# ScalarE reads two PSUM banks in VectorE's place, and the first expert's shares are applied later

## The chip, the core and the metric

The kernel runs on one core of a Trainium2 chip. The metric is the device time of one execution in microseconds; several executions are given by their median. The engines are named as in the profile: PE (TensorE, matrix products), ACT (ScalarE), DVE (VectorE), POOL (GpSimd) and SP (SyncE, which here only issues DMAs). PE writes its sums into banks of PSUM; ACT and DVE read them from there.

## What is computed

Three stages, all in fp32. An attention with 2 batches, 8 heads, 768 tokens and a mask from clusters; then a softplus layer; then 8 experts, whose outputs are weighted by shares P that Sinkhorn's iteration makes:

```python
x = attention(q, k, v, centroids)                 # 1536 x 512
h = x @ w_in                                      # 512 -> 2048
x = (np.maximum(h, 0.0) + np.log1p(np.exp(-np.abs(h)))) @ w_out
P = np.exp(logits - logits.max())                 # logits = x @ w_gate, 1536 x 8
for _ in range(8):
    P /= P.sum(1, keepdims=True) + 1e-09
    P /= P.sum(0, keepdims=True) + 1e-09
    P *= N / E
for e in range(E):
    out += P[:, e:e + 1] * (np.maximum(x @ w1[e], 0.0) @ w2[e])
```

## The kernel before

**Precision.** Every fp32 operand is split into a rounded high part and its residue (names ending in h and l: wh/wl for weights, gh/gl for activations, vh/vl for second weights). A product takes three matrix passes: high x high, and the two mixed ones. ACT makes the high part by a cast, DVE or POOL the residue by a subtraction.

**Attention** runs to about 290 us and isn't touched by the change.

**Softplus layer**, about 290 to 580 us. `m1` lists 16 units of two chunks of the hidden dimension for one batch. `plain_group` makes a unit's four sums of 128 x 384 in the banks la and lb in turn, so a bank is used again by the group after next. After each sum `act` (L665 on) makes softplus: Abs (L671) reads the bank, Exp (L672) and Ln (L673) work on that in SBUF, DVE's L674 adds max(h, 0), which it reads from the bank, and ACT and DVE split the result (L676, L677). `layer2` multiplies the unit before. `fetch_unit` and `to32` convert the weights from 64-bit words on ACT and DVE in between (L123 to L127).

**Experts**, from about 580 us. Sixteen blocks k = 0 to 15, batch k // 8, expert k % 8. Both layers use one level of Strassen's method with seven products (Winograd's form): `PROD` lists them as pairs of an input combination and a weight combination, and which of two running sums, "a" or "b", each adds to. `l1_group` makes layer 1's products: for each quarter u of the hidden dimension, seven groups i of six passes. The running sum is read out between products: after groups 0, 2 and 3 ACT copies the bank to SBUF (L925, tiles c0 and c2); after groups 1, 4 and 5 DVE's L935 adds one of these copies to the bank and writes a block of the hidden layer (A11, A22, A12); after group 6 ACT writes A21 with Relu (L933). Group 6 adds to the bank that group 4's sum was read from, with only group 5 between. Three banks, la, lb and y1, take turns.

`l2_piece` makes layer 2's products, seven i in two halves p of three pieces each, in the banks y0/y2, y3, y4, y5, and DVE adds the finished pieces, times the share, onto the output in `xt` (L967 for the first, L969 for the rest). `g_sum` and `g_split` make the combinations of the hidden layer (L72, L74) and their residues (L897); `w2_load` (SP), `w2_add` (POOL's DMA queue) and `w2_split` (L875, L876) those of the weights; `w1_load` and `w1_split` (L845, L846) do it for layer 1. `t_step` builds sums of weights for later experts by DMAs in the same blocks. `first_share` doesn't exist.

**Order.** All of the third stage is put on one list by `do(t, ...)`: t counts steps, a step being one layer 1 group, 28 (G1) to a block. Layer 2 of block k lies beside layer 1 of block k + 1, from S0 = 28 (k + 1) on. For k = 0 it starts LAG0 = 8 steps later and is packed into the 20 steps left, since its sums need the shares: Sinkhorn (`sinkhorn`, phase 0 the row sums on DVE, phase 1 the column sums by a product with ones on PE, L767, and its division on DVE) has its eight iterations at 5.5 + 4.2 it, phase 1 2.9 steps after phase 0. The list gives the program's order; the scheduler of the framework orders each engine's queue by it, moved ahead by `high_priority(n)`, and an engine works through its queue strictly in order.

Of the kernel before, what the change touches and what calls it, by code (L numbers as in the profile page):

```python
# [7 lines left out]
F32 = mybir.dt.float32  # L8
# [3 lines left out]
AF = mybir.ActivationFunctionType  # L12
ALU = mybir.AluOpType
# [7 lines left out]
def attention_moe_moe2(ctx, tc, v, qt, kt, centroids, w_in, w_out, w_gate, w1, w2, eye, out, dbg=None):  # L21
    nc = tc.nc
    B, H, S, D = v.shape
    NC_ = centroids.shape[1]
    N, DM = out.shape
    DFF = w_in.shape[1]
    E = w_gate.shape[1]
    FE = w1.shape[2]
    P = 128
    NT = S // P  # L30
    HT = NT // 2
# [14 lines left out]
    xt = [xp.tile([P, KC, S], F32, tag=f"x{b}", name=f"x{b}") for b in range(B)]  # L46
# [533 lines left out]
    c2 = prep_centroids()  # L580
# [8 lines left out]
    for i in range(NHALF):  # L589
        g = i // 4  # L590
        for t in range(HT):
            n = 6 * i + 2 * t - LEAD
# [6 lines left out]
        for s in range(NT):  # L599
            n = 6 * i + s  # L600
# [37 lines left out]
    ps_y = ctx.enter_context(tc.tile_pool(name="ps_y", bufs=1, space=PSUM))  # L638
# [28 lines left out]
    def act(u, q, cols, src):  # L667
        nm = f"{u[0]}{u[1]}_{u[2]}_{u[3]}_{q}{cols.start}"
        g = GF[u, q][:, cols]
        t = fp.tile([P, FH], F32, tag="u", name="u" + nm, bufs=2)  # L670
        nc.scalar.activation(t, src, AF.Abs)  # L671
        nc.scalar.activation(t, t, AF.Exp, scale=-1.0)  # L672
        nc.scalar.activation(t, t, AF.Ln, bias=1.0)  # L673
        nc.vector.scalar_tensor_tensor(g, src, 0.0, t, ALU.max, ALU.add)  # L674
        gh, gl = GT[u, q]
        nc.scalar.copy(gh[:, cols], g)  # L676
        nc.vector.tensor_tensor(gl[:, cols], g, gh[:, cols].bitcast(F32), ALU.subtract)  # L677
# [38 lines left out]
    Pt = mp.tile([P, B * NT, E], F32, tag="Pt", name="Pt", bufs=1)  # L716
    Nt = mp.tile([P, B * NT, E], F32, tag="Nt", name="Nt", bufs=1)
# [36 lines left out]
    def sinkhorn(it, ph):  # L754
        n = B * NT
        if ph == 0:
            rs = mp.tile([P, n], F32, tag="rs", name=f"rs{it}", bufs=1)
            nc.vector.tensor_reduce(rs, Pt, AX.X, ALU.add)
            nc.vector.tensor_scalar(rs, rs, 1e-9, None, ALU.add)
            nc.vector.reciprocal(rs, rs)  # L760
            nc.vector.tensor_tensor(Pt, Pt, rs.unsqueeze(2).to_broadcast([P, n, E]), ALU.mult)
            cs = G["cs"] = mp.tile([P, E], F32, tag="cs2", name=f"cs{it}", bufs=1)
            nc.vector.tensor_reduce(cs, Pt.rearrange("p t e -> p e t"), AX.X, ALU.add)
            return
        cs = G["cs"]
        cp = ps_y.tile([P, E], F32, tag=f"y{4 + it % 2}", name=f"cp{it}")
        nc.tensor.matmul(cp, ones_f, cs, start=True, stop=True)  # L767
        nc.vector.tensor_scalar(cs, cp, 1e-9, float(E) / N, ALU.add, ALU.mult)
        nc.vector.reciprocal(cs, cs)
        nc.vector.tensor_tensor(Pt, Pt, cs.unsqueeze(1).to_broadcast([P, n, E]), ALU.mult)  # L770
        if it == 7:
            nc.vector.tensor_scalar(Nt, Pt, -1.0, None, ALU.mult)
# [108 lines left out]
    def x_tile(k, name, p):  # L881
        t = XG[k, name, p] = gp.tile([P, 2, FH], F32, tag="X" + name, name=f"X{name}{k}_{p}", bufs=XB[name])
        return t
# [18 lines left out]
    def l1_group(k, u, i):  # L902
        xn, wn, bank = PROD[i]
        p, v = divmod(u, 2)
        nm = f"{i}m{k}_{u}"
        if i in (0, 1, 3):
            tag = ("la", "lb", "y1")[(4 * k + u + (0, 1, 0, 2)[i]) % 3]
            LB[bank] = (ps_y if tag == "y1" else ps_l).tile([P, FH], F32, tag=tag, name="l" + nm)
        ps = LB[bank]
        hi, lo = XC[f"2_{k // E}", xn]  # L910
        wh, wl, s_ = W1U[k, u][wn]
        n, nk = 0, KC // 2
        for k_ in range(nk):
            ks = slice(k_ * P, (k_ + 1) * P)
            for wt, xx in ((wh, hi), (wh, lo), (wl, hi)):
                nc.tensor.matmul(  # L916
                    ps, wt[:, s_, ks], xx[:, k_, :],
                    start=i in (0, 1, 3) and n == 0, stop=n == 3 * nk - 1, skip_group_check=True,
                )
                n += 1  # L920
        if i in (0, 2, 3):
            tag = "c2" if i == 2 else "c0"
            c = LB["c", i] = gp.tile([P, FH], F32, tag=tag, name=tag + nm, bufs=1)
            with tc.high_priority(40):
                nc.scalar.copy(c, ps)  # L925
            return
        name = {1: "A11", 4: "A22", 5: "A12", 6: "A21"}[i]
        if not v:
            x_tile(k, name, p)
        t = XG[k, name, p]  # L930
        with tc.high_priority(40):
            if i == 6:
                nc.scalar.activation(t[:, v], ps, AF.Relu)  # L933
            else:
                nc.vector.tensor_tensor(t[:, v], ps, LB["c", {1: 0, 4: 3, 5: 2}[i]], ALU.add)  # L935
        if v and i != 6:
            nc.scalar.activation(t, t, AF.Relu, scale=1.0 if name == "A11" else -1.0)  # L937

    def l2_piece(k, i, p, t):
        sb, e = divmod(k, E)  # L940
        ch = PROD[i][2]
        if p == 0 and t == 0 and i in (0, 1, 3):
            tags = ("y4", "y5") if ch == "b" else (("y0", "y2")[k % 2], "y3")
            YA[ch] = [ps_y.tile([P, 512], F32, tag=g, name=f"Y{ch}{n}m{k}_{i}") for n, g in enumerate(tags)]
        y = YA[ch]
        ps = y[t // 2][:, t % 2 * 256 : t % 2 * 256 + 256]
        (gh, gl), (wh, wl) = GH[k, i, p], WH[k, i, p]
        ts = slice(t * P, (t + 1) * P)
        for v in range(2):
            for n, (g, w) in enumerate(((gh, wh), (gh, wl), (gl, wh))):  # L950
                nc.tensor.matmul(  # L951
                    ps, g[:, v, ts], w[:, v, :],
                    start=i in (0, 1, 3) and p == 0 and v == 0 and n == 0 and t != 1,
                    stop=p == 1 and v == 1 and n == 2, skip_group_check=True,
                )
        if p == 0 or t == 0:
            return
        r, c = ((0, 0), (0, 0), (0, 1), (1, 1), (1, 1), (0, 1), (1, 0))[i]
        yv = xt[sb].rearrange("p k s -> p (k s)").rearrange("p (m d) -> p m d", d=DM)
        for t_ in ((0, 1) if t == 1 else (2,)):  # L960
            m = r * HT + t_
            src = y[t_ // 2][:, t_ % 2 * 256 : t_ % 2 * 256 + 256]
            acc = yv[:, m, c * 256 : (c + 1) * 256]
            scl = (Nt if c else Pt)[:, sb * NT + m, e : e + 1]
            with tc.high_priority(30):
                if e == 0 and i in (0, 2, 3, 6):
                    nc.vector.tensor_scalar(acc, src, scl, None, ALU.mult)  # L967
                else:
                    nc.vector.scalar_tensor_tensor(acc, src, scl, acc, ALU.mult, ALU.add)  # L969
            if e == E - 1 and i in (5, 6):  # L970
                nc.sync.dma_start(out.rearrange("(b p t) d -> b t p d", b=B, t=NT)[sb, m], yv[:, m])

    def xc_prep(sb, step):
        blk, mq = XBLK[sb], slot_pool["mq"]
# [32 lines left out]
    def do(t, fn, *args):  # L1007
        ev2.append((t, len(ev2), fn, args))

    G1, LAG0, SH = 28, 8, 7  # L1010
    split_at = {}
    t1 = [G1 * k + (SH if k >= E else 0) for k in range(NB)]
    for k in range(NB):
# [12 lines left out]
            for name, d in (("+S1", 14), ("+S2", 17), ("+S3", 20.4)):  # L1026
                do(t1[k] + d, xc_prep, 1, (name,))
        S0 = t1[k] + G1
        lag = LAG0 if k == 0 else 0
        sp = (G1 - lag) / 14  # L1030
        for p in range(2):
            r = t1[k] + 16 if p == 0 else S0 + 0.3
            for n, name in enumerate(("S1", "S2", "S3")):
# [1 line left out]
            do(S0 + 7 + 2 * p, g_sum, k, "S4", p)  # L1035
        first = split_at.setdefault(k, [])
        for j in range(14):
            t = S0 + lag + sp * (j - 3) + 0.2 if j >= 4 else S0 + 2 * j - 5.8
            first.append(max(t, t1[k] + 9))
        for i in range(7):  # L1040
            b, i_ = divmod(7 * k + i - 3, 7)
            t = split_at[b][2 * i_ + 1] + 0.15 if b >= 0 else -1
# [3 lines left out]
        for j in range(14):  # L1046
            i, p = divmod(j, 2)
            do(first[j], w2_split, k, i, p)
            do(first[j] + 0.1, g_split, k, i, p)
            for n in range(3):  # L1050
                do(S0 + lag + sp * j + sp * n / 3 + 0.01, l2_piece, k, i, p, n)
    for c, jobs in enumerate(JM):
        for j, job in enumerate(jobs):
            for n in range(len(STEPS[job[0]])):
                do(2 + 14 * c + 46 * j + 4.4 * n, behind_pe, t_step, ("gp", "wp")[c], *job, n)
    for hf in range(2):
        do(0.5 + hf, lambda hf=hf: gate(1, hf))
        do(2.5 + 1.5 * hf, lambda hf=hf: gate_max(hf))
    for it in range(8):
        for ph in range(2):  # L1060
            do(5.5 + 4.2 * it + 2.9 * ph, lambda it=it, ph=ph: sinkhorn(it, ph))

    tsum_at = {}
    for c, jobs in enumerate(JF):
# [83 lines left out]
```

## Time and profile before

| | us |
|---|---|
| median of 3 executions | 1584.24 |
| lowest, highest | 1583.39, 1588.66 |
| the profiled execution | 1580.72 |
| its span, first to last instruction | 1578.9 |
| PE busy in it | 1501.3 (95%) |
| DVE busy | 1237.9 (78%) |
| ACT busy | 1005.9 (64%) |
| POOL busy | 775.8 (49%) |

The profile is of one execution. Busy time of PE is modelled from overlapping passes, so it is read through its waits: an entry "X <- Y" says that engine X stood idle before an operation, and that Y's end released it. The granted clock is the share of PE's full speed; 1.00 is 2.4 GHz and 0.50 is 1.2 GHz. L numbers are lines of the kernel before. A name like l0m<-chS,wlCm says which tile is written from which.

### The profile page before, as it was taken

The numbers are of one execution on the slowest core, as the hardware profiler recorded it, in microseconds if no ns is written. First come the engines' busy times: TensorE is split into PE (matmuls) and PEld (weight loads), VectorE is DVE, ScalarE is ACT, GpSimd is POOL, SyncE is SP. The second block draws the span as 40 slices with busy tenths as digits, with TensorE's granted clock in tenths as the row PEclk, the third lists the DMA queues.
The fourth block names the chain that finished last, engine by engine and source line by source line (L and its number), as shares of the span: only waits on it lengthen the run. The fifth ranks groups of instructions, "written<-read, shape, count | busy, mean of one in ns | idle before, by whom it ended". The sixth has DMA issues, their size and how long they took to land. (4 is left out here: it accounts for less than half of the span.)

```text
span 1578.9 us, 26984 instructions
## 1 busy us (share of the span) xinstructions
PE 1501.3 (95%) x9873; PEld 1436.7 (91%) x9873; DVE 1237.9 (78%) x1826; ACT 1005.9 (64%) x1854; POOL 775.8 (49%) x570
## 2 busy tenths in 40 slices
PE   5889999899999998999999999999999999999998
PEld 4778888789999868999999999988999999999998
DVE  4899899876764538887887787898878878878868
ACT  4788888766665535566656656675566666666664
POOL 3322323433223325466665666575556656656655
PEclk7999999899999999999999999999999999999999
DMA  8555520388886618879889798635646546545524
GB/s 226 146 148 137 145 66 6 97 235 222 209 216 159 147 47 188 226 178 263 202 210 254 184 227 208 155 107 141 185 131 149 139 141 149 139 142 147 141 89 109
DMA packets 268533, 253.02 MB, mean 160 GB/s; under 512 B 12272, under 2 KB 235632, under 8 KB 268400
## 3 DMA queue, kind: packets, MB, share of 16 engines
q1 hardware_dynamic: 229984, 205.09, 43.1%
q0 software_dynamic: 38272, 46.14, 18.4%
q8 instruction: 77, 1.26, 0.3%
q14 instruction: 56, 0.46, 0.1%
q10 hardware_dynamic: 144, 0.07, 0.0%
HBM read 202.49 MB, written 28.31 MB: 146 GB/s over the span
## 5 line engine op out<-in xcount | busy, mean ns | idle before, releaser
L876 POOL TENSOR_TENSOR vl<-w2r,vh 128x512 fp32r<-128x512 f32 x224 | 382.4, 1718 | 338.0 <-ACT vh L875 319.3
L897 DVE TENSOR_TENSOR gl<-XA,gh 128x768 fp32r<-128x768 f32 x160 | 165.5, 1036 | 80.1 <-ACT gh L896 79.5
L896 ACT CAST gh<-XA 128x768 fp32r<-128x768 f32 x160 | 133.9, 837 | 96.8 <-PE Ya1m L951 87.2
L875 ACT CAST vh<-w2r 128x512 fp32r<-128x512 f32 x224 | 137.6, 615 | 23.2 <-DMA w2r<-in_moe_w_dram 11.5
L951 PE MATMUL Ya0m<-vh,gl 128*128 128x256 f32 x512 | 144.3, 282 | 1.6 <-DVE gl L897 1.6
L951 PE MATMUL Ya0m<-vh,gh 128*128 128x256 f32 x512 | 144.1, 281 | 0.4 <-ACT gh L896 0.4
L951 PE MATMUL Ya0m<-vl,gh 128*128 128x256 f32 x512 | 144.0, 281 | 0.0
L554 DVE TENSOR_TENSOR el<-t,eh 128x384 fp32r<-128x384 f32 x192 | 102.5, 548 | 11.8 <-ACT eh L550 10.6
L951 PE MATMUL Yb0m<-vh,gh 128*128 128x256 f32 x384 | 109.1, 284 | 1.1 <-DVE x L969 1.1
L951 PE MATMUL Yb0m<-vh,gl 128*128 128x256 f32 x384 | 109.3, 285 | 0.4 <-DVE gl L897 0.4
L951 PE MATMUL Yb0m<-vl,gh 128*128 128x256 f32 x384 | 109.2, 284 | 0.4 <-POOL vl L876 0.4
L515 DVE TENSOR_REDUCE sc<-s 128x1 f32<-128x768 f32 x96 | 91.1, 950 | 21.3 <-PE s L507 21.1
L550 ACT CAST eh<-t 128x384 fp32r<-128x384 f32 x192 | 91.2, 480 | 23.9 <-PE t L547 13.4
L937 ACT ACTIVATE XA<-XA 128x768 f32<-128x768 f32 x96 | 81.3, 848 | 35.4 <-DVE XA L935 35.4
L547 PE MATMUL t<-idf,E 128*128 128x128 f32 x576 | 98.7, 279 | 4.7 <-ACT OHT L455 2.8
L951 PEld LDWEIGHTS Ya0m<-vh,gl 128*128 128x128 f32 x512 | 97.1, 190 | 1.8 <-DVE gl L897 1.8
L951 PEld LDWEIGHTS Ya0m<-vh,gh 128*128 128x128 f32 x512 | 96.8, 189 | 0.7 <-ACT gh L896 0.7
L520 ACT ACTIVATE E<-s,sc 128x768 f32<-128x768 f32 x96 | 87.1, 908 | 16.0 <-DVE sc L515 15.1
L951 PEld LDWEIGHTS Ya0m<-vl,gh 128*128 128x128 f32 x512 | 96.8, 189 | 0.0
L72 DVE TENSOR_TENSOR XS<-XA,XA 128x768 f32<-128x768 f32 x32 | 64.0, 2001 | 31.4 <-ACT XA L933 31.4
L547 PEld LDWEIGHTS t<-idf,E 128*128 128x128 f32 x576 | 73.5, 143 | 14.5 <-ACT OHT L455 3.6
L896 ACT CAST gh<-XS 128x768 fp32r<-128x768 f32 x64 | 53.4, 836 | 47.7 <-PE Yb1m L951 34.9
(253 smaller groups left out, 5334.2 us busy)
## 6 DMA issues: line engine op xcount, KB each, us to landing
w2r<-in_moe_w_dram SPq DMA_DIRECT2D x84, 512.0 KB, 4.6
ts<-in_moe_w_dram POOLq DMA_DIRECT2D x44, 512.0 KB, 8.0
w2r<-in_moe_w_dram POOLq DMA_DIRECT2D x44, 512.0 KB, 8.3
td<-ts SPq DMA_DIRECT2D x40, 512.0 KB, 6.7
wf<-td SPq DMA_DIRECT2D x64, 256.0 KB, 3.7
w2r<-td SPq DMA_DIRECT2D x32, 512.0 KB, 4.0
w1r<-td SPq DMA_DIRECT2D x64, 256.0 KB, 3.5
AT<-HL SPq DMA_DIRECT2D x64, 192.0 KB, 3.8
```

Source lines behind the costliest of these rows:

```text
L72: eng.tensor_tensor(out_, a, b, op)
L515: nc.vector.tensor_reduce(SC[i][:, 0, j, t : t + 1], Et[i, t][:, :, 0:CB], AX.XY, ALU.max, negate=True)
L520: nc.scalar.activation(e.rearrange("p (a c) -> p a c", a=2), Et[i, t][:, :, 0:CB], AF.Exp, bias=sc[:, 0, j, t : t + 1], scale=1.0, accum_o ...
L547: nc.tensor.transpose(pt[:, t * P : (t + 1) * P], Et[i, t][:, s * P : (s + 1) * P], idf)
L550: nc.scalar.copy(eh, TT[i, s])
L554: nc.vector.tensor_tensor(el, TT.pop((i, s)), EHL[i, s].bitcast(F32), ALU.subtract)
L875: nc.scalar.copy(h, src)
L876: nc.gpsimd.tensor_tensor(l, src, h.bitcast(F32), ALU.subtract)
L896: nc.scalar.copy(h, src)
L897: nc.vector.tensor_tensor(l, src, h.bitcast(F32), ALU.subtract)
L937: nc.scalar.activation(t, t, AF.Relu, scale=1.0 if name == "A11" else -1.0)
L951: nc.tensor.matmul(ps, g[:, v, ts], w[:, v, :], start=i in (0, 1, 3) and p == 0 and v == 0 and n == 0 and t != 1, stop=p == 1 and v == 1 a ...
```

## The change

Three edits. In `act`, ACT takes max(h, 0) from the bank by Relu right after Abs, and DVE adds two tiles of SBUF. In `l1_group`, ACT also copies the bank of group 4 to SBUF, into a new tile c4, and DVE adds c4 and c0, without the priority of 40. In the third stage's list, layer 2 of block 0 loses its lag, expert 0's pieces in batch 0 are summed without shares, `first_share` multiplies the sums by the shares in four calls of three multiplications from step 56.6 on, Sinkhorn's iterations lie 6.2 steps apart with phase 1 4.2 steps after phase 0, and its column sums use bank y2 instead of y4 and y5 in turn.

```diff
@@ act
         nc.scalar.activation(t, src, AF.Abs)
+        nc.scalar.activation(g, src, AF.Relu)
         nc.scalar.activation(t, t, AF.Exp, scale=-1.0)
         nc.scalar.activation(t, t, AF.Ln, bias=1.0)
-        nc.vector.scalar_tensor_tensor(g, src, 0.0, t, ALU.max, ALU.add)
+        nc.vector.tensor_tensor(g, g, t, ALU.add)
@@ sinkhorn
-        cp = ps_y.tile([P, E], F32, tag=f"y{4 + it % 2}", name=f"cp{it}")
+        cp = ps_y.tile([P, E], F32, tag="y2", name=f"cp{it}")
@@ l1_group
-        if i in (0, 2, 3):
-            tag = "c2" if i == 2 else "c0"
+        if i in (0, 2, 3, 4):
+            tag = ("c0", "", "c2", "c0", "c4")[i]
             c = LB["c", i] = gp.tile([P, FH], F32, tag=tag, name=tag + nm, bufs=1)
             with tc.high_priority(40):
                 nc.scalar.copy(c, ps)
-            return
+            if i != 4:
+                return
+            ps = c
...
-        with tc.high_priority(40):
+        with tc.high_priority(0 if i == 4 else 40):
@@ l2_piece
-                if e == 0 and i in (0, 2, 3, 6):
+                if k == 0 and i in (0, 2, 3, 6):
+                    nc.vector.tensor_copy(acc, src)
+                elif k == 0:
+                    nc.vector.tensor_tensor(acc, src, acc, ALU.add)
+                elif e == 0 and i in (0, 2, 3, 6):
                     nc.vector.tensor_scalar(acc, src, scl, None, ALU.mult)
@@ new
+    def first_share(r, c):
+        yv = xt[0].rearrange("p k s -> p (k s)").rearrange("p (m d) -> p m d", d=DM)
+        for m in range(r * HT, (r + 1) * HT):
+            acc = yv[:, m, c * 256 : (c + 1) * 256]
+            nc.vector.tensor_scalar(acc, acc, (Nt if c else Pt)[:, m, 0:1], None, ALU.mult)
@@ the list
-    G1, LAG0, SH = 28, 8, 7
+    G1, SH = 28, 7
...
-        lag = LAG0 if k == 0 else 0
-        sp = (G1 - lag) / 14
+        sp = G1 / 14
...
-            t = S0 + lag + sp * (j - 3) + 0.2 if j >= 4 else S0 + 2 * j - 5.8
+            t = S0 + sp * (j - 3) + 0.2 if j >= 4 else S0 + 2 * j - 5.8
...
-                do(S0 + lag + sp * j + sp * n / 3 + 0.01, l2_piece, k, i, p, n)
+                do(S0 + sp * j + sp * n / 3 + 0.01, l2_piece, k, i, p, n)
...
+    for n, q in enumerate(((0, 0), (0, 1), (1, 1), (1, 0))):
+        do(56.6 + 2.4 * n, first_share, *q)
...
-            do(5.5 + 4.2 * it + 2.9 * ph, lambda it=it, ph=ph: sinkhorn(it, ph))
+            do(5.5 + 6.2 * it + 4.2 * ph, lambda it=it, ph=ph: sinkhorn(it, ph))
```

## Rows read from the trace of the kernel before

**Rows 1.** The page's first part: busy time, share of the span, instructions.

```profile
PE 1501.3 (95%) x9873; PEld 1436.7 (91%) x9873; DVE 1237.9 (78%) x1826; ACT 1005.9 (64%) x1854; POOL 775.8 (49%) x570
```

**Rows 2.** Waits of PE, whole span: released by, us in total, times, longest us.

```profile
PE l0m L916 <- DVE XA L935: 14.2, 10, 2.9
...
PE p L660 <- DVE gf L674: 7.1, 5, 3.0
...
PE l0m L916 <- POOL wlCm L846: 3.6, 2, 2.6
...
PE cp L767 <- DVE cs L763: 2.4, 2, 1.4
```

**Rows 3.** Windows: busy PE, PEld, DVE, ACT, POOL; PE's granted clock; DMA share, GB/s.

```profile
301.03:311.27 10.24, 8.67 (x24) 6.90 (x25) 8.75 (x14) 7.86 (x18) 5.32 (x4) 0.50 0.96 236
...
857.40:860.81 3.41, 3.35 (x12) 3.35 (x13) 2.50 (x5) 1.03 (x3) 0.63 (x2) 0.50 1.09 367
```

**Rows 4.** Timeline around 857 us: start, duration, instruction, [idle before it and releaser].

```profile
851.09 0.34 PE L916 MATMUL l0m<-chS,wlCm 128*128 128x384 f32 x1
...
854.51 0.83 ACT L896 CAST gh<-XA 128x768 fp32r<-128x768 f32 x1 [2.68 <-PE Ya1m L951]
...
856.84 0.56 DVE L935 TENSOR_TENSOR XA<-l0m,c03m 128x384 f32<-128x384 f32 x1
...
857.46 0.69 PE L916 MATMUL l0m<-chA,whCm 128*128 128x384 f32 x1 [2.86 <-DVE XA L935]
```

**Rows 5.** Timeline from 546 to 555 us, softplus layer.

```profile
546.28 0.48 ACT L671 ACTIVATE u<-p 128x384 f32<-128x384 f32 x1
...
553.03 0.55 DVE L674 SCALAR_TENSOR_TENSOR gf<-p,u 128x384 f32<-128x384 f32 x1
...
553.64 0.69 PE L660 MATMUL p<-chA,whA 128*128 128x384 f32 x1 [2.97 <-DVE gf L674]
```

**Rows 6.** Timeline, start of the softplus layer.

```profile
302.41 0.69 PE L660 MATMUL p<-clA,whA 128*128 128x384 f32 x1 [0.51 <-POOL clA L106]
...
342.86 0.44 PE L660 MATMUL p<-chA,whA 128*128 128x384 f32 x1 [1.52 <-DVE gf L674]
```

**Rows 7.** Windows by stage, columns as in rows 3.

```profile
290.00:553.00 263.00, 255.19 (x1430) 237.27 (x1430) 173.97 (x279) 162.24 (x317) 90.48 (x65) 0.98 0.75 193
613.00:660.00 47.00, 42.38 (x263) 40.59 (x264) 39.30 (x74) 27.00 (x46) 23.66 (x18) 0.96 1.03 247
660.00:1040.00 380.00, 370.47 (x2609) 368.87 (x2608) 311.59 (x395) 234.78 (x395) 233.11 (x157) 0.99 0.80 204
1040.00:1160.00 120.00, 111.46 (x778) 109.23 (x777) 103.19 (x123) 75.89 (x127) 71.49 (x46) 1.00 0.54 146
```

**Rows 8.** Groups of DVE, 290 to 580 us: busy us, mean ns | idle before, releaser.

```profile
L677 DVE TENSOR_TENSOR gl<-gf,gh 128x384 fp32r<-128x384 f32 x64 | 43.4, 677 | 21.6 <-ACT gh L676 21.5
L674 DVE SCALAR_TENSOR_TENSOR gf<-p,u 128x384 f32<-128x384 f32 x64 | 35.4, 555 | 53.3 <-ACT u L673 53.1
```

**Rows 9.** Tile c22m, the copy after group 2: who waited for it (us, times).

```profile
  PEld l0m L916: 0.6, 3
```

**Rows 10.** Waits of PE, 660 to 1040 us, then 1040 to 1160 us.

```profile
PE l0m L916 <- DVE XA L935: 9.4, 4, 2.9
...
PE l0m L916 <- DVE XA L935: 3.7, 4, 1.6
```

**Rows 11.** DVE and ACT operations in SBUF; durations ns min/median/max, or a group.

```profile
L72 DVE TENSOR_TENSOR XS<-XA,XA x32: 944/2260/4096, 604.4 to 1543.0; 128x768 f32<-128x768 f32 x32
...
L967 DVE TENSOR_SCALAR x<-Ya0m,Pt x8: 467/474/485, 642.1 to 1187.6; 128x256 f32<-128x256 f32 x8
...
L772 DVE TENSOR_SCALAR Nt<-Pt 128x96 f32<-128x96 f32 x1 | 1.9, 1933 | 0.0
...
L937 ACT ACTIVATE XA<-XA 128x768 f32<-128x768 f32 x96 | 81.3, 848 | 35.4 <-DVE XA L935 35.4
```

**Rows 12.** Timeline, POOL's queue before chunk C's residues in block 1.

```profile
641.95 1.28 POOL L216 DMA_DIRECT2D w2r<-in_moe_w_dram  x1 [13.33 <-DMA ts<-in_moe_w_dram]
```

## The prediction

> **What bounds the kernel now.** I read the page first. TensorE (PE) is busy 95% of the span [rows 1], so the time can only move by what PE loses. Then I listed who PE waits for. Only two large entries lie behind the attention, and both name a bank of PSUM that VectorE (DVE) has still to read [rows 2]: the group of layer 1 that follows the A22 sum waits 14.2 us for L935, and the softplus layer waits 7.1 us for L674. Two smaller ones belong to the first blocks of the last stage: 3.6 us for GpSimd's (POOL's) residues of chunk C, and 2.4 us for the column sums of Sinkhorn. Third came the granted clock in short windows. After a long wait of PE it stands at 0.50, the lower of its two levels (1.2 GHz), for 3.41 us; there are four such stretches after the attention, from 553.62, 645.78, 857.40 and 922.26, each begun by a PE wait of 2.6 to 3.0 us. A fifth lasts 10.24 us from 301.03 [rows 3]. At half speed, 3.41 us do the work of 1.70, so each of the four costs 1.70 us and the fifth 5.1. The shorter waits between 660 and 1160 us show none behind them.
>
> Last I read the timeline at one wait of each kind. At 857 us, PE had finished the A22 group at 851.4 and had other work until 854.6. DVE, in order, reached the sum only at 856.84, and PE went on at 857.46 after 2.86 us [rows 4]. ACT (ScalarE) had meanwhile idled 2.68 us before a cast at 854.51. At 553 us it is the same: ACT read the bank by 546.8 (Abs), but Exp, Ln and then DVE's turn came first, and DVE read it at 553.03; PE lost 2.97 us [rows 5].
>
> **Basis of the sum.** The rows are from one execution of 1580.72 us (span 1578.9, the rest lies around it). That is 3.5 us under the median of 1584.24, and under the lowest of the three. The sum below is a difference against that execution; the forecast is this difference set against the median, since a median is what is predicted.
>
> **Part 1, softplus.** ACT's new Relu follows Abs at once, so a bank is free some 1 us after PE ends (two reads of 0.48 [rows 5]), without waiting for Exp, Ln and DVE. Removed: 2.97 us at 553 with its 1.70 of half clock, 1.52 us at 342.86 [rows 6], and two waits of 0.2; together 6.6 us. The fifth wait, 2.15 us at 301.24, I don't count: right behind it PE stands for POOL's residue of the input at 302.41 [rows 6], which is no earlier for this change, so PE would only stand there longer. Nor do I count the 5.1 us of clock there. Added: 64 Relus of 0.48 us, 30.7 us of ACT, in a stretch where ACT is busy 162 of 263 us [rows 7]; it becomes 73%, and hides. Behind each Relu queue Exp, Ln and the weight casts, all 0.48 us later. Layer 2 runs one unit behind and covers that; only the first unit has no such cover, so I charge 0.5 us. DVE's addition keeps its 0.56 us but now has both inputs in SBUF; the row of the same shape with two SBUF inputs has a mean of 677 ns against 555 [rows 8]: 64 x 0.12 = 8 us more of an engine that is busy 174 of 263 us. Net gain 6.1 us; the ends are -1 (the waits become waits for ACT) and 13 (the start is freed too).
>
> **Part 2, A22.** The sum's bank is now read by an ACT copy that comes before the add. PE's cover between this group and the next of that bank was 3.2 us at 857 (851.4 to 854.6). The nearest row for the new wait is the copy of group 2, the same shape, engine, priority and bank, with one group between: over its 64 cases PE stood 0.6 us for it [rows 9]. Removed: 9.4 us in four waits between 660 and 1040 us, all of the sort shown above [rows 4], and two half-clock stretches, 3.4 us. Between 1040 and 1160 there are 3.7 us more [rows 10], but DVE is busy 103 of 120 us there [rows 7] and PE also waits for it elsewhere, so I take half, 1.9. Sum 14.7, less 0.6 for the new waits: 14.1. What it costs elsewhere: ACT gets 64 x 0.48 = 31 us over 1000 us (62% busy becomes 65% [rows 7]). The add loses its priority and has both inputs in SBUF. Its extra lies between 0.12 us, as above, and 1.3 us, as for the 128x768 differences (944 ns at least, 2260 in the median [rows 11]): 8 to 84 us of DVE over 960. DVE is at 82% between 660 and 1040 [rows 7] and can take it, but queued behind it are the sums that free other banks, so I charge one more wait of the mean size of the four, 2.0 us. I take this low value since the add is short and nearest to the row of its own shape. Net gain 12.1; the ends are 4 and 17.
>
> The row on L72 shows DVE stretched to twice its shortest time while L674, with an input in PSUM, keeps its 555 ns [rows 8, 11]. The Trainium skill, "SBUF — State Buffer", section "Who interferes with whom", says that a DVE instruction with two SBUF inputs contends with a GpSimd instruction that reads SBUF, and that the later one blocks. It speaks against moving these operands out of PSUM: by it the adds stand at the upper end, and with a wait of 2.0 us in four blocks instead of one the sum below would be 1567.1; by the row of the same shape it stays at 1561.1.
>
> **Part 3, layer 2 of the first expert, Sinkhorn.** Without the lag, layer 2 of block 0 spreads over 28 steps instead of 20, starting 8 steps earlier. With it move its g and w2 splits (ACT, POOL, DVE) and five weight loads on SP, up to 7 steps earlier past w1 loads and stores of the sums; two additions by POOL's queue keep their steps. PE's work stays the same. Today's losses from 580 to 660: 2.4 us for Sinkhorn's column sums, 3.6 for POOL's residues and 1.70 of clock, 1.1 for L935; together 8.8. A column sum now has 4.2 steps instead of 2.9 for its row half, and two of eight waited: I leave 0.8. L935's 1.1 goes with part 2's copy. Of the POOL waits, the short one (1.0) goes, since the steps around it get longer. The long one (2.6 and the clock) comes from POOL standing 13.33 us in its queue for a landing [rows 12] while the DMA engines' share is 1.03 [rows 7]; bytes don't change, only their order, so I take half, 2.2. Gain 1.6 + 1.1 + 1.0 + 2.2 = 5.9; ends 0 and 8.8. Column sums move to bank y2, which layer 2 first takes for expert 1, from step 56 on; Sinkhorn ends at step 53. Evacuating without shares costs what it did, an instruction for an instruction. Added: 12 multiplications by shares on DVE. They lie between 0.47 us (the same shape from PSUM) and 1.93 us (a smaller one from SBUF) [rows 11]: 6 to 23 us of DVE beside PE's work, in groups of three. A group of 1.4 us is covered by PE's 3 us, one of 5.8 isn't: I charge 1.0, ends 0 and 8.
>
> **Sum.** 6.1 + 12.1 + 5.9 - 1.0 = 23.1 us gained: 1584.2 - 23.1 = 1561.1 us.
>
> **The rivals.**
> A, the freed waits return on DVE: it is busy 82 to 86% from 660 to 1160, and a PE that isn't held meets the residues of layer 2 or the sums of another bank. For it: such waits stand between 1040 and 1160 already. Against: between 660 and 1040 the list has none [rows 10]. It leaves the clock and half of the waits, about 10 us: 1574.
> B, slower: DVE's adds, now with two SBUF inputs, stretch; ACT stands for them at L937 (35.4 us already [rows 11]), and ACT's queue, which now holds one more of PE's banks, holds PE. One such wait as at 857, with its clock, is 4.6 us. It decides from the sixth of the 16 blocks on (6 x 4.6 exceeds 23.1 + 2.0 charged); in eleven of them the time is 1584.2 - 25.1 + 50.6 = 1610, in eight 1596. Against: ACT idled 2.7 us next to the wait [rows 4].
> C, the copy doesn't come in time: placed behind the cast at 854.51, it ends 0.5 us after 855.34 and PE still waits 1.4 of the 2.86 us. Half of the 9.4 us stays, the clock is gained: 1566. So the change doesn't do all it says.
> D, the start of the softplus layer is freed too, with its 2.15 and 5.1 us: 1554.
> E, the order of the queues falls so that gain and loss cancel, with block 1's loads late: within 4.75 us of 1584.
>
> **How the numbers follow.** A measurement of this kernel tells about 0.3% (4.75 us) from no change. Forecast 0.48 (1555 to 1567), C 0.10, D 0.12, A 0.13: together 0.83 faster. E has 0.09. B has 0.08, for the trace bears out that such DVE operations stretch but not that PE waits for them. The range takes the forecast, C, D and A, and leaves out the outer ends and B: 1548 to 1578.
>
> **What would show it.** Right: L935 and the softplus sum vanish from what PE waits for; the half-clock stretches at 553, 857 and 922 are gone; PE's waits for L925's copies stay under 2 us; no wait for column sums over 1 us. Part 2's charge shows in the mean of the A22 add, 0.7 us or more. Wrong: new PE waits for L969, L897 or ACT of over 2.5 us with a half clock behind them, or a wait in block 1 for loaded weights.

## The result, and the profile after

The changed kernel takes 1570.61 us (median of four, 1568.54 to 1573.25) beside 1583.82 us for the kernel before (four, 1582.25 to 1588.66): a ratio of 0.9911, with an interval of 0.9891 to 0.9931. It is 14.1 us faster, by the interval 10.9 to 17.3; 23.1 were forecast. The profiled execution took 1568.54 us, its span is 1566.7.

From the page's first part, PE still fills the span, and DVE, ACT and POOL are all busier than in [rows 1], POOL without one instruction more:

```profile
PE 1492.8 (95%) x9873; PEld 1433.2 (91%) x9873; DVE 1260.6 (80%) x1838; ACT 1043.1 (67%) x1982; POOL 792.1 (51%) x570
```

The waits of PE from 280 to 570 us (total, times, longest), beside the softplus line of [rows 2]:

```profile
PE y L695 <- ACT gh L677: 6.1, 2, 4.9
PE p L660 <- ACT gf L672: 2.8, 2, 2.3
...
```

And from 570 to 1160 us, beside [rows 10]:

```profile
PE l1m L917 <- DVE XA L938: 6.8, 4, 4.3
PE Ya1m L954 <- DVE x L976: 4.9, 1, 4.9
PE l0m L917 <- ACT c00m L926: 3.0, 2, 2.7
PE Ya1m L954 <- DVE x L970: 1.9, 1, 1.9
PE l3m L917 <- ACT c03m L926: 1.2, 1, 1.2
PE l0m L917 <- ACT c22m L926: 0.9, 1, 0.9
```

Both old entries, softplus's DVE sum and L935 ahead of l0m, are gone (L938 is the changed kernel's line for L935, and L926 for L925, L954 for L951, L976 for L969). PE now waits in other places, and most of these waits again name DVE; L938 itself still holds PE ahead of the bank of l1m.

Groups of DVE, 570 to 1570 us (busy us, mean ns | idle before), say why. The A22 sum, 0.55 us while it read a bank, now takes 0.79; the residues of L898 lasted 165.5 us in the kernel before (1.04 each) and now last 187.1. First the two lines of the kernel before, then of the kernel after:

```profile
L897 DVE TENSOR_TENSOR gl<-XA,gh 128x768 fp32r<-128x768 f32 x160 | 165.5, 1036 | 80.1 <-ACT gh L896 79.5
...
L935 DVE TENSOR_TENSOR XA<-l0m,c03m 128x384 f32<-128x384 f32 x64 | 35.2, 549 | 8.9 <-PE l0m L916 7.2
```

```profile
L898 DVE TENSOR_TENSOR gl<-XA,gh 128x768 fp32r<-128x768 f32 x160 | 187.1, 1171 | 50.5 <-ACT gh L897 50.5
...
L938 DVE TENSOR_TENSOR XA<-c44m,c03m 128x384 f32<-128x384 f32 x64 | 50.6, 790 | 9.0 <-ACT c44m L926 7.5
```

A table by stage shows where the time went. Each figure (us) is the distance between the first l0m matmuls of successive blocks in a trace; the attention ends at its last matmul. e8, e10 and e12 are experiments told below.

```
                 attention  softplus  block 0  block 1  2 to 6  7 to 8  9 to 14  rest
before             289.0     291.7     42.4     66.2    309.3   126.5    357.7   96.0
after              285.7     289.7     44.1     60.7    304.6   130.0    353.9   98.0
e8 (part left out) 285.0     290.3     44.0     60.1    295.0   122.1    354.0   94.2
e10                284.9     291.0     44.8     60.1    295.0   124.9    353.9   93.6
e12 (on before)    285.8     291.4     42.2     66.5    295.5   126.0    355.8   93.7
```

In before and e12 one l0m matmul of block 9 runs some 1.1 us ahead of the others, so that their figure for 7 to 8 is that much shorter, and the one for 9 to 14 longer, than in the other rows. The attention isn't touched. Over the traces of all runs it varies from 284.3 to 289.5 us: besides the one at its start, the kernel before had three half-clock stretches there, the one after a single one, and that makes 3.3 of the 12.2 us between the two spans. Of the other 8.9, softplus gives 2.0, blocks 0 and 1 give 3.8, and all that follows 3.0. The profiled execution of the kernel before lay 3.1 us under its median, so the stages add up to less than the 14.1 us of the medians.

### The profile page after: what moved, and what is told of

Read it like the earlier page. It is cut to its first block, busy times and chain, and to the rows that moved or that the text cites. A ratio compares the mean times of both kernels' runs of the same rounds, so it can differ in the third digit from the quotient of the medians.

```text
span 1566.7 us, 27092 instructions
## 1 busy us (share of the span) xinstructions
PE 1492.8 (95%) x9873; PEld 1433.2 (91%) x9873; DVE 1260.6 (80%) x1838; ACT 1043.1 (67%) x1982; POOL 792.1 (51%) x570
## 4 chain that ended last, share of the span: by engine, by line
PE 77%; DVE 13%; ACT 4%; DMA 3%; issue 3%; POOL 1%; SPq 0%; DVEq 0%; ACTq 0%; POOLq 0%
PE l0m L917 15%; PE Ya0m L954 10%; PE l3m L917 8%; PE Yb0m L954 7%; PE y L695 7%; PE p L660 6%; PE Ya1m L954 5%; PE l1m L917 4%; PE Yb1m L954 4%; PE av L562 3%; PE s L507 3%; PE t L547 2%; DVE gl L898 1%; DVE el L554 1%; DVE sc L515 1%
## 5 line engine op out<-in xcount | busy, mean ns | idle before, releaser
L877 POOL TENSOR_TENSOR vl<-w2r,vh 128x512 fp32r<-128x512 f32 x224 | 390.6, 1750 | 330.3 <-ACT vh L876 324.8
L898 DVE TENSOR_TENSOR gl<-XA,gh 128x768 fp32r<-128x768 f32 x160 | 187.1, 1171 | 50.5 <-ACT gh L897 50.5
L897 ACT CAST gh<-XA 128x768 fp32r<-128x768 f32 x160 | 133.9, 837 | 37.4 <-PE Ya1m L954 29.3
L954 PE MATMUL Ya0m<-vh,gh 128*128 128x256 f32 x512 | 145.3, 284 | 1.4 <-ACT vh L876 1.4
L954 PE MATMUL Ya0m<-vl,gh 128*128 128x256 f32 x512 | 145.1, 283 | 1.0 <-POOL vl L877 1.0
L954 PE MATMUL Ya0m<-vh,gl 128*128 128x256 f32 x512 | 145.2, 284 | 0.0
L954 PE MATMUL Yb0m<-vh,gl 128*128 128x256 f32 x384 | 108.2, 282 | 0.0
L954 PE MATMUL Yb0m<-vh,gh 128*128 128x256 f32 x384 | 108.2, 282 | 0.0
L954 PE MATMUL Yb0m<-vl,gh 128*128 128x256 f32 x384 | 108.1, 282 | 0.0
L954 PEld LDWEIGHTS Ya0m<-vh,gh 128*128 128x128 f32 x512 | 97.9, 191 | 1.6 <-ACT vh L876 1.6
L954 PEld LDWEIGHTS Ya0m<-vl,gh 128*128 128x128 f32 x512 | 97.8, 191 | 1.2 <-POOL vl L877 1.2
L954 PEld LDWEIGHTS Ya0m<-vh,gl 128*128 128x128 f32 x512 | 98.1, 192 | 0.0
L72 DVE TENSOR_TENSOR XS<-XA,XA 128x768 f32<-128x768 f32 x32 | 60.0, 1876 | 32.0 <-ACT XA L936 32.0
L897 ACT CAST gh<-XS 128x768 fp32r<-128x768 f32 x64 | 53.6, 837 | 40.9 <-PE Yb1m L954 33.3
```

The source lines that it names most:

```text
L877: nc.gpsimd.tensor_tensor(l, src, h.bitcast(F32), ALU.subtract)
L897: nc.scalar.copy(h, src)
L898: nc.vector.tensor_tensor(l, src, h.bitcast(F32), ALU.subtract)
L954: nc.tensor.matmul(ps, g[:, v, ts], w[:, v, :], start=i in (0, 1, 3) and p == 0 and v == 0 and n == 0 and t != 1, stop=p == 1 and v == 1 a ...
```

## The experiments

**Theory 1** is that the change removes the old waits as forecast, and that DVE then comes late at other sums, since it stands behind POOL whenever it reads two operands from SBUF while POOL reads there too. Rivals: the copies of ACT or the lost priority of the A22 sum are what is late, or the shares cost it.

**The parts alone.** e1 has only the softplus edit, e2 only the A22 edit with its priority, e3 the rest (no lag, shares later, Sinkhorn stretched, y2); e4 is the whole change again, on the same chip.

> Only the softplus edit (Relu by ACT). Theory 1, from the stages of the two profiles (292.2 us before, 290.1 after): the waits at 342 and 553 shrink, but the first unit now waits some 5 us for the cast behind four Relus and loses its clock too; gain 2 us, ratio 0.9985. Rival, the prediction's part 1 as written: 6 us, ratio 0.996.

> Only the ACT copy of group 4's bank. Theory 1: PE's waits for L935 after group 4 vanish, but the add with two SBUF inputs has a mean near 0.79 us instead of 0.55, and DVE operations with two SBUF inputs behind a row of POOL operations hold other banks; net gain 5 to 8 us, ratio 0.996. Rival, the prediction's part 2: 12 us, ratio 0.992.

> Only the first expert's later shares, no lag, and the longer Sinkhorn; group 4's bank read by DVE as before. Theory 1: gain 4 us, ratio 0.9975, with one wait of 3 to 5 us near 610 us that Sinkhorn's operation in DVE's queue causes, and one near 685 us behind the multiplications by shares. Rival, that this part loses what the others win: 0 or slower, ratio 1.000 to 1.003.

> The changed kernel again, on the same chip as the three parts. Theory 1: ratio 0.991, and the three parts' gains add up to it within 3 us. Rival, that the parts are tied through the order of the queues: the sum is off by 5 us or more.

Beside 1583.38 us for the kernel before, measured: e1 1580.72 (ratio 0.9985, 0.9969 to 1.0), e2 1577.43 (0.9959, 0.9938 to 0.998), e3 1583.23 (1.0002, 0.9985 to 1.0019), e4 1570.95 (0.9926, 0.9902 to 0.9951). By these ratios the gains alone are 2.4, 6.5 and 0 us, together some 9; the whole change gains 11.7 by its ratio and 12.4 by the medians. The 3 us between lie inside the intervals of the four runs, so the times alone don't show that the parts are tied, and e3 missed the 4 us expected of it. The traces show it: block 1 takes 65.2, 67.9 and 66.6 us with one part each (66.2 before) and 60.7 with all. That is where parts 2 and 3 need one another. Waits of PE in e2, 570 to 660 us, then in e3, 570 to 720 us:

```profile
PE cp L767 <- DVE cs L763: 9.1, 3, 4.6
...
```

```profile
PE l0m L916 <- DVE XA L935: 7.5, 4, 2.9
...
PE cp L767 <- DVE cs L763: 0.2, 1, 0.2
```

With the copy alone, PE reaches Sinkhorn's column sums (four steps behind their row half only with part 3) before DVE has done them; with the stretched Sinkhorn alone, it still stands for the A22 bank. Each part uncovers what the other removes.

**The multiplications by shares (e5).** They are moved from DVE to ACT.

```diff
-            nc.vector.tensor_scalar(acc, acc, (Nt if c else Pt)[:, m, 0:1], None, ALU.mult)
+            nc.scalar.activation(acc, acc, AF.Identity, scale=(Nt if c else Pt)[:, m, 0:1])
```

> The changed kernel, with the 12 multiplications by shares on ACT instead of DVE. Theory 1: they are what holds the evacuation L970 that PE waits 1.86 us for at 685 us (with a half-clock stretch behind it); without them in DVE's queue blocks 1 and 2 together (123.4 us in the changed kernel) take 120. Rival: DVE would be late there anyway, 123.

In the kernel after, the wait at 685 us (timeline) stands right behind four multiplications on DVE:

```profile
681.62 3.74 DVE L984 TENSOR_SCALAR x<-x,Nt 128x256 f32<-128x256 f32 x4
...
685.28 0.41 DVE L970 COPY x<-Ya1m 128x256 f32<-128x256 f32 x1
685.75 0.39 PE L954 MATMUL Ya1m<-vh,gh 128*128 128x256 f32 x1 [1.86 <-DVE x L970]
```

e5 took 1571.24 us (before, beside it: 1584.86). e5 to e9 are single executions, and those of the changed kernel alone lie between 1568 and 1575, so e5, e6 and e7 are read by their waits. The wait at 685 us is gone, and one of 1.9 us for XA stands at 730 us in its place; blocks 1 and 2 together take 122.4 us, 1.0 less than after and nearer to the rival's 123 than to the 120 expected. The multiplications cause this wait, but taking them off DVE mostly moved it.

**The priority (e6).**

```diff
-        with tc.high_priority(0 if i == 4 else 40):
+        with tc.high_priority(40):
```

> The changed kernel, with the priority of 40 given back to the A22 add. Theory 1: the add's lateness is of no account for PE, every block stays within 0.5 us and the wait of 4.9 us at 1050 us too. Rival B of the prediction (ACT stands for the add at the Relu of A22 and holds PE's banks): the 4.9 us shrink by over 2 and blocks 7 and 8 together (130 us) by 3.

1569.42 us, with the large waits in the same places (5.0 us for L976, 4.3 for the sum at 613 us, 2.9 for c00m) and one more of 1.7 us for L938 at 704 us. Blocks stay within 1.3 us, not within the 0.5 expected, in both directions. Neither of the falls that rival B asked for came: the lost priority isn't what costs.

**The first softplus unit (e7).** Its sum and cast were to go ahead of DVE's conversions.

```diff
-        nc.vector.tensor_tensor(g, g, t, ALU.add)
...
-        nc.scalar.copy(gh[:, cols], g)
+        with tc.high_priority(40 if u == m1[0] else 0):
+            nc.vector.tensor_tensor(g, g, t, ALU.add)
+            nc.scalar.copy(gh[:, cols], g)
```

> The changed kernel, with priority for the softplus sum and the cast of the first unit. Theory 1: the wait of 4.9 us at the first layer 2 is the old limit in a new place: DVE's queue, where 10 conversions of weights stand ahead of the first sum; with the sum ahead of them it goes, and the softplus stage falls from 289.7 to 286 us. Rival: the inputs' residues on POOL hold PE then, and the stage stays at 289 to 290.

1572.11 us; the wait stayed at 4.93. But the edit didn't do what it was for: the sum still stands behind the conversion of L127 in DVE's queue. This run tells nothing of what the start would give with the sum earlier; that stays open.

**POOL without its reads (e8, e9).** e8 is the changed kernel, e9 the kernel before, each with the residue of the experts' second weights put to zero, so POOL issues as many instructions there but reads nothing.

```diff
-        nc.gpsimd.tensor_tensor(l, src, h.bitcast(F32), ALU.subtract)
+        nc.gpsimd.memset(l.bitcast(F32), 0.0)
```

> The changed kernel, where POOL fills the residues of the second weights with zeros instead of subtracting: this leaves out the low part of the experts' second weights, and takes away 224 POOL operations that read SBUF. Theory 1: DVE operations with two SBUF inputs stand behind POOL's reads; the A22 add falls from 0.78 to under 0.62 us, the residues L898 from 1.17 to under 1.0, and PE's waits for DVE and ACT from 660 to 1040 us (6 us) to under 1. Rival: the add's length comes from its inputs in SBUF alone and stays over 0.75, and PE's waits stay.

> The kernel before, with POOL filling the second weights' residues with zeros (their low part left out, as in the run of the changed kernel that gained 24 us by it). Theory 1: the waits for L935 that the change removes came from DVE standing behind POOL's reads; without these they go as well, each block from 2 on takes 59.2 us, and the time falls to 1556 to 1564, so that the change is worth only some 12 us of softplus and first blocks on top. Rival: PE waits for DVE's place in the order whatever POOL does; at least half of the 13 us of these waits stay, and the time stays over 1572.

e8 takes 1546.48 us (1584.86 beside it), 24 less than the changed kernel. Its DVE groups from 570 to 1545 us, the same two as above:

```profile
L898 DVE TENSOR_TENSOR gl<-XA,gh 128x768 fp32r<-128x768 f32 x160 | 155.3, 971 | 98.8 <-ACT gh L897 98.2 <-PE Yb1m L954 0.3
...
L938 DVE TENSOR_TENSOR XA<-c44m,c03m 128x384 f32<-128x384 f32 x64 | 38.1, 596 | 22.6 <-ACT c44m L926 21.0
```

Both shrink, by 0.2 us each, though DVE's own work is the same. From 660 to 1040 us PE has one wait left, of 1.8 us for L976 (under 1 us was expected); it lies at 1036.8 us, in block 7. Blocks 2 to 6 take 59.0 us each. e9 takes 1554.68 us, somewhat under the range expected, and after 660 us it has no wait for L935 at all: the waits that the change was made against were themselves DVE standing behind POOL.

POOL also has less to do in e8 and e9, so the times alone don't separate its reads from its load. The trace of e8 does, since it holds both kinds of POOL work. Its timeline, DVE beside a subtraction and beside a fill:

```profile
1029.92 2.38 POOL L1009 TENSOR_TENSOR clS<-xS,chS 128x768 fp32r<-128x768 f32 x1
1030.50 2.22 DVE L938 TENSOR_TENSOR XA<-c44m,c03m 128x384 f32<-128x384 f32 x1
...
1033.51 0.53 POOL L877 MEMSET vl<- 128x512 f32 x1 [1.21 <-PE Ya1m L954]
1033.72 0.94 DVE L898 TENSOR_TENSOR gl<-XA,gh 128x768 fp32r<-128x768 f32 x1
```

Counted over the expert stage of e8, for the DVE sums and differences with two inputs in SBUF: of 39 that begin during a POOL subtraction (0.1 us or more before its end), 35 last over 0.15 us longer than the shortest of their kind, by up to 1.7 us. Of 30 that begin during a fill with no subtraction beside them, and of 50 during POOL's issue of a DMA, none lasts longer by more than 0.05 us. In the kernel after, all 18 A22 sums that overlap a POOL subtraction are stretched, begin after it and end 0.41 or 0.42 us behind its end; the other 46 take 0.56 at most. Of the 128 sums that read a bank, 92 overlap one too, and none takes more than 0.56. So it is POOL's subtractions, which read SBUF, that hold DVE, and only where DVE has both inputs there.

The mechanism can be seen one instruction at a time. Timeline of the kernel after, 835 to 845 us, first POOL:

```profile
835.67 1.30 POOL L216 DMA_DIRECT2D w2r<-in_moe_w_dram  x1 [2.60 <-PE l1m L917]
836.48 2.35 POOL L847 TENSOR_TENSOR wlCm<-wf,whCm 128x768 fp32r<-128x768 f32 x1
838.31 3.00 POOL L877 TENSOR_TENSOR vl<-w2r,vh 128x512 fp32r<-128x512 f32 x2
840.79 1.68 POOL L216 DMA_DIRECT2D ts<-in_moe_w_dram  x1
```

Then the other engines:

```profile
835.93 6.21 DVE L898 TENSOR_TENSOR gl<-XA,gh 128x768 fp32r<-128x768 f32 x1
...
842.85 0.54 DVE L938 TENSOR_TENSOR XA<-l1m,c00m 128x384 f32<-128x384 f32 x1
...
843.48 0.48 ACT L926 COPY c03m<-l3m 128x384 f32<-128x384 f32 x1 [3.30 <-DVE XA L938]
...
844.01 0.45 PE L917 MATMUL l3m<-chS,whCm 128*128 128x384 f32 x1 [1.19 <-ACT c03m L926]
```

A residue with two SBUF inputs, 0.97 us long on average in e8, lasts 6.21 us: it ends at 842.14, 0.83 us after the last of POOL's three subtractions (841.31). The sum from the bank behind it keeps its 0.54, but it comes late; ACT's copy waits for that sum, and PE for the copy. PE's wait names ACT, two steps from its cause.

**The same work on DVE (e10, e11, e12).** If so, DVE should do these subtractions itself, with the full result. e10 does it on the changed kernel, e11 for half of them (`nc.vector if p else nc.gpsimd`), e12 on the kernel before.

```diff
-        nc.gpsimd.tensor_tensor(l, src, h.bitcast(F32), ALU.subtract)
+        nc.vector.tensor_tensor(l, src, h.bitcast(F32), ALU.subtract)
```

> The changed kernel, with all residues of the second weights made by DVE instead of POOL; the result is the full one. Theory 1 (POOL's reads are what slows DVE): DVE gets 224 x 0.68 = 152 us and loses some 125 us of standing; busy 862 of 970 us, and PE's waits from 660 to 1040 us fall below 2 us, but in blocks 7 and 8 DVE is the bound; 1555 to 1566 us, ratio 0.985. Rival: DVE is too full, PE waits for it everywhere; 1585 or more.

> The changed kernel, with every second residue of the second weights on DVE and the others on POOL. Theory 1: half of POOL's reads go, and with them about half of the standing; 1558 to 1567 us, ratio 0.987, near the run with all of them on DVE but easier in blocks 7 and 8. Rival: DVE meets POOL as often, only with more work of its own; 1571 or more, ratio 0.992 or more.

> The kernel before, with all residues of the second weights made by DVE instead of POOL: the one-word edit without the change. Theory 1: POOL's reads were the cause of the waits for L935 too, so most of the gain comes without the change; 1556 to 1563 us, ratio 0.984, some 8 us above the changed kernel with the same edit (1550.3), which is what the softplus and first-block edits are then worth. Rival: DVE, now busy near 87%, is late at group 4's bank again, and only ACT's copy makes the edit possible; 1568 or more, ratio 0.990 or more, with waits for L935 of 10 us or more after 660 us.

e10 takes 1550.32 us beside 1584.2 (ratio 0.9788, 0.9762 to 0.9814), e11 1558.61 (0.9833, 0.9806 to 0.986), e12 1561.3 beside 1585.73 (0.9844, 0.983 to 0.9858). e10 beats both kernels. Its page row, the new group of DVE, and PE's waits from 570 to 1160 us:

```profile
PE 1488.8 (96%) x9873; PEld 1430.6 (92%) x9873; DVE 1266.6 (82%) x2062; ACT 1045.4 (68%) x1982; POOL 412.5 (27%) x346
```

```profile
L877 DVE TENSOR_TENSOR vl<-w2r,vh 128x512 fp32r<-128x512 f32 x224 | 164.7, 736 | 3.6 <-ACT vh L876 3.6
```

```profile
PE l1m L917 <- DVE XA L938: 4.4, 1, 4.4
PE Ya1m L954 <- DVE x L976: 4.2, 1, 4.2
PE l0m L917 <- ACT c00m L926: 0.3, 1, 0.3
...
```

DVE took on 224 instructions and 164.7 us and is busy 6 us longer than in the kernel after: what it no longer loses behind POOL pays for them. The waits in blocks 2 to 6 are gone. Those at 611 and 1050 us stay, so these 224 subtractions don't make them; but both stand behind DVE operations that are stretched beside other subtractions of POOL, as is shown below for each.

The change is still worth 9 to 11 us on top: e10 and e12 ran on different chips, and their times differ by 11.0 us, their ratios by 8.9 and their two traces by 8.7. In the table block 1 gains 6.4 and block 0 loses 2.6, blocks 7 to 14 gain 3.0; the A22 bank in blocks 2 to 6 no longer counts (295.5 and 295.0).

## Why the prediction was right, and where its sizes were off

The sign was right, and the range held the time, but only since it took in rival A: 1570.6 lies outside the 1555 to 1567 on which the forecast had put 0.48. The forecast was 9.5 us too low: the old waits went for the most part, and each of the three parts brought new ones that the sum had priced too low. By the stages of the two profiled executions: softplus 2.0 us instead of 6.1, blocks 0 and 1 3.8 instead of 4.9, all later work 3.0 instead of 12.1.

**Part 1.** The step that failed first is "only the first unit has no such cover, so I charge 0.5 us". Start of the softplus layer, timeline of after:

```profile
297.26 0.69 DVE L127 SCALAR_TENSOR_TENSOR wf<-r,wf 128x512 int32<-128x512 int32 x1
...
297.87 0.55 DVE L675 TENSOR_TENSOR gf<-gf,u 128x384 f32<-128x384 f32 x1
...
298.45 0.51 ACT L677 CAST gh<-gf 128x384 fp32r<-128x384 f32 x1 [4.59 <-DVE gf L675]
...
302.71 0.51 ACT L677 CAST gh<-gf 128x384 fp32r<-128x384 f32 x1
...
303.28 1.01 PE L695 MATMUL y<-gh,w2h 128*128 128x512 f32 x2 [4.94 <-ACT gh L677]
```

PE isn't held at the bank any more, reaches layer 2 sooner and stands there 4.94 us. The first sum comes behind DVE's conversions, ACT stands 4.59 us for it, and the second cast ends at 303.22. The half clock around this wait (from 301.12 us) still lasts 6.83 us where it lasted 10.24 [rows 3]. At 553 us too, the reasoning that Relu "follows Abs at once" failed. ACT's queue before that wait:

```profile
542.00 0.49 ACT L671 ACTIVATE u<-p 128x384 f32<-128x384 f32 x1
...
547.12 0.83 ACT L104 CAST chS<-xS 128x768 fp32r<-128x768 f32 x1 [0.80 <-DVE xS L74]
547.86 0.86 ACT L672 ACTIVATE gf<-p 128x384 f32<-128x384 f32 x2
```

Between Abs and Relu lie 5.4 us, the last of it a cast that waits for DVE. PE's wait fell from 2.97 [rows 5] to 2.3 us only. The half clock behind it is gone in this trace, but stands again in those of e5, e6 and e7, so those 1.70 us can't be counted on.

**Part 2.** The step that failed is the low value: "I charge one more wait of the mean size of the four, 2.0 us". That charge took 0.12 us for a sum's extra; it is 0.24 (0.79 less 0.55), 15 us in all. The view of tile c44m (ns: shortest, median, longest) shows that it falls on a few of the 64, with up to 1.1 us each, which a price for each sum hides:

```profile
L938 DVE TENSOR_TENSOR XA<-c44m,c03m x64: 542/548/1652, 588.1 to 1523.5; 128x384 f32<-128x384 f32 x64
```

And the residues of L898, which the sum didn't contain, lengthened by 21.6. The forecast mark, a mean of 0.7 us or more, was met. New waits behind such stretched work are 1.19, 1.86 and 0.93 us in blocks 4 and 5; then come two, in blocks 7 and 8, with a half clock in them. Windows of the latter (columns as [rows 3]):

```profile
1048.64:1055.47 6.83, 5.15 (x24) 5.15 (x25) 6.00 (x10) 4.76 (x8) 5.33 (x2) 0.50 0.10 28
1065.71:1069.12 3.41, 2.89 (x10) 2.89 (x11) 2.42 (x4) 2.72 (x6) 2.89 (x2) 0.50 1.11 190
```

Against the 59.0 us that a block takes without waits in e8, blocks 2 to 6 now lose 9.6 us instead of 14.3, and blocks 7 and 8 lose 12.0 instead of 8.5 (9.6 with the 1.1 us told at the table). Those 12.0 are the waits of 4.94 and 2.71 and half of 6.83 and of 3.41, 12.8, within 1 us. The wait at 1050 us stays in e6 (5.0) and e10 (4.2), so neither the priority nor these residues on POOL make it. In the kernel after, DVE's queue ahead of it holds two operations of 0.95 us stretched to 2.62 and 2.04, beside POOL's subtractions of L1009 and L877 (timeline):

```profile
1040.36 2.68 POOL L1009 TENSOR_TENSOR clS<-xS,chS 128x768 fp32r<-128x768 f32 x1 [1.46 <-ACT chS L1008]
1041.23 2.62 DVE L898 TENSOR_TENSOR gl<-XA,gh 128x768 fp32r<-128x768 f32 x1
...
1043.78 2.04 DVE L1009 TENSOR_TENSOR clS<-xS,chS 128x768 fp32r<-128x768 f32 x1
```

In e8, where one operation loses 1.7 us there, the wait is 1.8 us. So part of the lateness is the same standing behind POOL, by subtractions that no run took away; how much, stays open. The wait of 2.71 us at 1066 is of another kind: the copy that PE waits for stands in ACT's queue behind a cast that had waited 6.56 us for a load of w2r.

The Trainium skill, "SBUF — State Buffer", section "Who interferes with whom", stands beside this: DVE with two SBUF inputs contends with a GpSimd operation that reads SBUF, and the later one blocks. The trace agrees: the A22 sum went from 0.55 to 0.79 us when its operand left PSUM and is at 0.60 in e8, while the neighbouring sum with one operand in PSUM kept its 0.54; and all 18 stretched A22 sums began after POOL's subtraction. (The order isn't always so plain: the record of the 6.21 us begins 0.55 us before POOL's first subtraction.) The 1567.1 us that the prediction worked out by it was nearer to the 1570.6 than the forecast, though it got there with a wait of 2.0 us in each of four blocks, and the waits came in fewer places and bigger.

**Part 3.** Alone it gave nothing (e3) where 4.9 us were counted; with part 2 in place block 1 became 5.5 us shorter. What failed is counting it by itself ("L935's 1.1 goes with part 2's copy" was the only tie seen). POOL's 2.6 us and their clock went, as did the column-sum waits of over 1 us. Two new waits took some back, the 1.86 us at 685 shown above and this one (timeline):

```profile
607.51 2.43 POOL L847 TENSOR_TENSOR wlCm<-w1r,whCm 128x256 fp32r<-128x256 f32 x2
607.84 2.23 DVE L762 TENSOR_TENSOR Pt<-Pt,rs 128x96 f32<-128x96 f32 x1
609.99 0.55 DVE L938 TENSOR_TENSOR XA<-c44m,c03m 128x384 f32<-128x384 f32 x1
...
610.63 0.48 ACT L926 COPY c00m<-l0m 128x384 f32<-128x384 f32 x1 [3.50 <-DVE XA L938]
610.70 0.54 DVE L938 TENSOR_TENSOR XA<-l3m,c22m 128x384 f32<-128x384 f32 x1
...
611.29 0.44 PE L917 MATMUL l1m<-chA,whAm 128*128 128x384 f32 x1 [4.33 <-DVE XA L938]
```

A Sinkhorn multiplication of 96 elements takes 2.23 us, where the shortest of its kind takes 0.24, ahead of the sum that frees l1m's bank. It too reads two tiles of SBUF, and ends 0.13 us behind POOL's subtractions for chunk C. These aren't among the 224 of w2, and the wait is there in e8 (4.3) and e10 (4.4) too; no run took them away.

**The rivals.** A's mechanism, freed waits that return on DVE, is what came: the time lies 9.5 us above the forecast, A lay 12.9 above it (1574). B, slower through L937 and ACT, didn't come at its price: PE has no wait for the new copies c44m, and e6 leaves the priority without effect. Its path shows once, at 919 us: ACT stood 4.81 us for DVE at the changed kernel's line for L937, and the copy behind held PE for 0.93 us. C is denied where it was placed: at 857 us the copy comes in time. D came in part: the start's half clock is 3.41 us shorter, but PE stands 4.94 us for layer 2 in it. E didn't either; loads in block 1 are not late.

Of the marks set, these held: the softplus sum is gone from PE's list, 857 and 922 have full clock, the column sums wait under 1 us. L935 is gone ahead of l0m but, as L938, holds l1m for 6.8 us. "Waits for L925's copies under 2 us" held except for one of 2.71. The mark of a wrong forecast, a new wait of over 2.5 us for L969, L897 or ACT with a half clock, came three times: 4.94 us for ACT's cast at 303 us, 4.94 for DVE's L976 (L969 before) at 1050 and 2.71 for ACT's copy at 1066.

## What to carry to other kernels

A wait of PE for one bank can be a symptom: compare the shortest and the mean duration of the instructions that the late engine did before it, and look at which other engine's reads of SBUF run beside the stretched ones. Moving operands out of PSUM freed a bank here, but exposed the engine that adds them to POOL's reads; a word that moved 224 subtractions from POOL to DVE gave more (24 us on the kernel before, 20 on the changed one) than the whole change. And parts that free one another's queues are priced together, since each alone may show nothing.

## What was not expected of the hardware

One DVE subtraction, 0.97 us long elsewhere, took 6.21 us while POOL went through three subtractions in a row (836.48 to 841.31 us): the end of the first did not set it free, and it ended 0.83 us after the last, while POOL was still issuing a DMA (to 842.47). Moving 164.7 us of subtractions onto DVE left its busy time in the expert stage nearly unchanged (836 us of 991 in the kernel after, 841 of 972 in e10). And the untouched attention varied by 5 us between traces, with one to three half-clock stretches besides the one at its start: a third of a change of this size, so that stages are compared, not spans.
